# Query projections in two alternating banks, and five loads behind the last output turn of a seam, in a fused transformer block

## The chip, the cores and the metric

The kernel runs on one core of a Trainium2 chip. The metric is device time in microseconds for one execution; the median over several runs is compared. Beside the runs there is one profiled execution, from which all views of the trace come.

## The reference

One transformer block on 2048 tokens of width 1024, in bf16, conditioned by a vector `c` (adaptive layer norm):

```python
mod = (silu(c) @ w_mod).reshape(1, 6, 1, -1)
sa, ca, ga, sb, cb, gb = (mod[:, i] for i in range(6))
h = layernorm(x) * (1 + ca) + sa
x = x + ga * attention(h)        # q = h @ wq, 32 heads of 128; 4 K/V heads, last 512 cached positions; then @ wo
h = layernorm(x) * (1 + cb) + sb
return x + gb * ((silu(h @ w_gate) * (h @ w_up)) @ w_down)     # width 3584 inside
```

## The kernel before

**Stages.** Tokens are cut into four chunks of 512. A start part computes the first two modulation vectors, the first chunk's layer norm and its first queries. Then comes the attention loop over `i`, the running number of chunk and head (128 in all, 32 to a chunk), and at the end of each chunk its output projection. The feed-forward part follows, chunk by chunk. Every instruction is issued from one Python program in the order in which its calls stand; each engine, and SyncE as issuer of nearly all DMAs, works through its own instructions in that order. A small tracker adds the semaphore waits: an instruction waits for the last writer of what it reads, and for the last writer and the readers of what it overwrites. So a DMA written earlier in the program is issued earlier by SyncE, and one that waits holds up all behind it.

**One step of the attention loop.** In step `i` the queries of head `i + 3` are projected (`qproj`, eight matmuls of 512 columns, L672), the scores of head `i - 1` are computed (four matmuls), and the value product of head `i - 2` (`pv`). `qproj` writes PSUM bank `QB` (4); VectorE then copies the bank to SBUF (the CAST, L679). Scores use banks 0 to 3, value products 5 and 6, and bank 7 is `XB`. After `pv` VectorE scales the output (L870, L873) and SyncE transposes it by DMA into `oT_all` (L876); this is called the output's turn. From head 34 on every second head, the even ones, takes another way: scores with queries on the partitions (`nat_scores`, L913 on ScalarE), a normalisation on VectorE (`nat_norm`, L919, L923), a transposing DMA of the probabilities (`nat_turn`, L929) and a value product two steps later (`nat_pv`, copied out by ScalarE, L940).

**The seam.** In the step in which the last head of a chunk is turned (`i` = 33, 65, 97), `oproj` runs the chunk's output projection: eight pieces `k` of 32 matmuls, one for each head, each piece in one of two banks and followed by a residual on VectorE (`resid`, L954 and L956). Piece 0 first takes heads 0 to 23, then the waiting value products, then heads 24 to 31 of the chunk; so head 31's turn has to have landed for the last matmul of piece 0. Into the pieces the first scores of the next chunk are slipped (`between`).

**Late modulation.** The modulation vectors of the feed-forward part are computed one column group at a time: `load_mt(m)` (L597) brings a transposed slice of `w_mod` into one of four slots, `mod_col(m)` (L604, VectorE) multiplies it with the condition and sums. There are 24 such slices. `late_col(m)` is `mod_col(m)` followed by `load_mt(m + 4)`, which has to wait for the slot. The first four loads stand in the table `LOADT` (step: slice), two columns are taken in steps 32 and 33, and `late_cols(k)` takes the rest between the output pieces of chunk 0.

**Other loads on SyncE.** `load_wq` (L363) brings 1 MB of query weights for four heads, `load_x` (L308) 1 MB of tokens for a chunk, by the table `LOADX`.

Of the kernel before, what the change touches and what calls it, by code (L numbers as in the profile page):

```python
# [130 lines left out]
def bass_adaLN_cond__sliding_block_cached__swiglu_ffn__prompt_kernel(  # L131
# [17 lines left out]
    Hq = HD // Dh  # L149
# [112 lines left out]
    QB = 4  # L262
    SCB = 0
    PVB = 5
    XB = 7

    with nc.Block() as block:

        @block.gpsimd
        def _(g):  # L270
# [36 lines left out]
            def load_x(ch):  # L307
                T.op(Q_x[TPC + ch], lambda: SP.dma_start(  # L308
                    x_res[:, ch * TPC:(ch + 1) * TPC, :],
                    xf[ch * CH:(ch + 1) * CH, :].rearrange("(t p) d -> p t d", p=P)),  # L310
                     writes=B_x[ch * TPC:(ch + 1) * TPC])
# [273 lines left out]
            NMT = 4  # L585
# [6 lines left out]
            def load_mt(m):  # L592
                sl = m % NMT
                n = L_ORDER[m]
                if mt[sl] is None:
                    mt[sl] = arena.at(OFF_HT + 2 * sl * KB, [D], BF16, [B_mt[sl]])
                T.op(Q_mt[sl], lambda: SP.dma_start_transpose(  # L597
                    mt[sl].rearrange("p (a b) -> p a b", a=1), w_mod[:, (NF + n) * P:(NF + n + 1) * P]),
                     writes=[B_mt[sl]])
# [8 lines left out]
            def late_col(m):  # L608
                mod_col(m)
                if m + NMT < NL:  # L610
                    load_mt(m + NMT)

            def late_cols(k):
                if k < 7:
                    for m in range(3 * k + (3 if k else 2), 3 * k + 6):
                        late_col(m)
                if k == 3:
                    T.op(DVE, lambda: V.tensor_copy(mstg[:, 0:DT], mcol[:, 2 * DT:3 * DT]), reads=[B_mcol], writes=[B_mstg])
                    row_turn()
                if k == 4:  # L620
                    row_put(2, mrow[0:DT, :], B_mrow)
                if k == 5:
                    row_get(2, rowb[1][:, :], B_row[1])
                if k == 6:
                    for g0 in range(2):
                        mod_take(g0, B_late[g0 + 1])
                    mod_gain(1, B_late[2], B_g[1])
                    for b_ in B_hT[0]:
                        for m_ in B_mt:
                            b_.absorb(m_)  # L630
# [23 lines left out]
            LEAD = 3  # L654
# [8 lines left out]
            def q_slot(i):  # L663
                return NQT + i % 2 if i < NQ0 else i % NQT
# [11 lines left out]
            def qproj(i, b=QB, k0=0):  # L676
                qproj_mm(i, b, k0, DT)
                qs = q_slot(i)
                T.op(DVE, lambda: V.tensor_copy(qT_s[qs], bank(b)), writes=[PB[b], B_qT[qs]])  # L679
# [279 lines left out]
            def oproj_mm(ch, k, b, h0, h1):  # L959
                j, hf = divmod(k, 2)  # L960
                for h in range(h0, h1):
                    mm(bank(b), oT_all[:, h, j * P:(j + 1) * P], wo_s[h // 4][:, h % 4, hf * 512:(hf + 1) * 512],
                       h == 0, h == Hq - 1, [B_wo[h // 4], B_oT[h]], PB[b])
# [6 lines left out]

            def oproj(ch, between, last):
                for k in range(2 * TPC):
                    b = [QB, XB][k % 2]
                    if k == 0:
                        oproj_mm(ch, k, b, 0, Hq - 8)
                        for n in last:
                            nat_pv(n)
                    oproj_mm(ch, k, b, 0 if k else Hq - 8, Hq)
                    oproj_end(ch, k, b)
                    if k < len(between):  # L980
                        between[k]()
                    if ch == 0:
                        late_cols(k)

            ln1 = {}
            ln2 = {}
# [10 lines left out]
                ln2[ch] = ln_task(ch, h2s[s], B_h2[s], 1, 3 * DT, B_late[1])  # L997
                bg.append(ln2[ch])

            LOADX = {19: 2, 2 * Hq + 1: 3}  # L1000
            GATEP = {4: (0, 1), 5: (2,), 6: (3,), 7: (4,), 9: (5,), 10: (6,), 12: (7,), 13: (8,), 15: (9,)}
            GATER = {19 + n: NGP + n for n in range(DT - NGP)}
            GATET = {23: 0, 24: 1}
            GATES = {26: 0, 27: 1}
            PUTT = {22: (0, c_sil, B_csil), 30: (1, mrow[0:DT, :], B_mrow)}
            GETT = {25: (0, sc_row, B_scr), 31: (1, rowb[0][:, :], B_row[0])}
            LOADT = {29: 0, 30: 1, 31: 2, 32: 3}
            LOADO = {5 + (21 * p) // 8: p for p in range(8)}
            LOADK = {1: 1, 5: 2, 6: 3}
            PTAT = {NAT0: OFF_H20, 3 * Hq: OFF_HT}  # L1010
            for i in range(1, NA + 2):
                ch, h = divmod(i, Hq)
                if i in LOADK:
                    load_k(LOADK[i])
                if i == 4:
                    load_wq((i + 4) // 4 + 1)
                if 2 <= i < NQ0:
                    q_shifted(i)
                if i in (2, 3):
                    load_wga(i - 2)  # L1020
                if i in LOADX:
                    load_x(LOADX[i])
                if i in LOADO:
                    load_wo(LOADO[i])
                if i in GATET:
                    gate_turn(GATET[i])
                if i == 28:
                    row_turn()
                if i in PUTT:
                    row_put(*PUTT[i])  # L1030
                if i in GETT:
                    row_get(*GETT[i])
                if i == 7:
                    add_ln1(1)
                if h == 2 and 1 <= ch < NCH - 1:
                    add_ln1(ch + 1)
                if h == 2 and ch == NCH - 1:
                    add_ln2(0)
                if i + LEAD < NA:
                    if (i + LEAD) % Hq == 0:  # L1040
                        finish(ln1[(i + LEAD) // Hq])
                    if i == 1:
                        scores(0)
                    if i in (1, 3, 5):
                        q_bias_mm(i + 1, i + 3, XB)
                    if i > NQ0:
                        qproj(i + LEAD)
                    elif i % 2 == 1:
                        qproj_mm(NQ0 + i // 2, QB, 0, HK)
                    else:  # L1050
                        qproj(NQ0 - 1 + i // 2, QB, HK)
                if i % 4 == 0 and i > NAT0:
                    load_wq(i // 4 + 2)
                if i in (Hq, Hq + 1):
                    late_col(i - Hq)
                n = i - (NA - LEAD)
                if 0 <= n <= 2:
                    oproj_mm(NCH - 1, 0, QB, 8 * n, 8 * n + 8)
                elif n >= 3:
                    oproj_mm(NCH - 1, 1, XB, 8 * (n - 3), 8 * (n - 3) + 8)  # L1060
                seam = (i - 1) % Hq == 0 and i + 1 in NAT
                if i + 1 in PTAT and not seam:
                    pt_region(PTAT[i + 1])
                if i in NAT and (i - 2) % Hq:
                    nat_norm(i, 1)
                nat = i % 2 == 1 and i + 1 in NAT
                if nat and not seam:
                    run_bg(1)
                    nat_scores(i + 1)
                if 1 <= i - 1 < NA and i - 1 not in NAT:  # L1070
                    scores(i - 1)
                if 0 <= i - 2 < NA:
                    if i - 4 in pt_of:
                        nat_pv(i - 4)
                    if i in NAT and (i - 2) % Hq:
                        nat_turn(i)
                    if i - 2 not in NAT:
                        pv(i - 2)
                    if nat and not seam:
                        nat_norm(i + 1, 0)  # L1080
                    ch2, h2 = divmod(i - 2, Hq)
                    if i % 4 == 1 and 5 < i < NAT0:
                        load_wq((i + 4) // 4 + 1)
                    if i in LOADT:
                        load_mt(LOADT[i])
                    if h2 == Hq - 1 and ch2 < NCH - 1:
                        oproj(ch2, [lambda: nat_scores(i + 1), lambda: (nat_norm(i + 1, 0), nat_norm(i + 1, 1))],
                              [n for n in sorted(pt_of) if n // Hq == ch2])
                        if seam:
                            if i + 1 in PTAT:  # L1090
                                pt_region(PTAT[i + 1])
                            nat_turn(i + 1)
                if not nat or seam:
                    run_bg(1)
                for n in GATEP.get(i, ()):
                    gate_part(n)
                if i in GATER:
                    gate_row(GATER[i])
                if i in GATES:
                    gate_sum(GATES[i])  # L1100
                if i == max(GATER):
                    gate_split()
# [107 lines left out]
            for jf in range(NCH * FT):  # L1210
                ch, ft = divmod(jf, FT)
# [45 lines left out]
```

## Time and profile before

| what | us |
|---|---|
| median of three runs | 1270.74 |
| lowest, highest | 1270.41, 1272.22 |
| profiled execution | 1270.27 |
| its span, first to last instruction | 1268.4 |
| outside the span | 1.9 |
| TensorE busy | 1261.8 |
| VectorE, ScalarE, GpSimd busy | 519.9, 392.9, 56.3 |

Busy times are sums over the span and say nothing of where an engine stands still. A row of the timeline gives start, length, engine, line, operation and count of instructions merged into one stretch, and in brackets the idle time before it with what ended it. SPq is the issuing of DMAs by SyncE: its length is the issue, not the transfer. A window's row gives, after its length, each engine's busy time with the count of instructions, then the granted clock of TensorE (1.00 is full speed), the DMA share and GB/s.

### The profile page before, as it was taken

How to read it: one execution, taken by the hardware profiler on the slowest of the kernel's cores; microseconds unless marked ns; L12 is line 12 of the kernel's file. 1: busy time of each engine (PE TensorE's matmuls, PEld its weight loads, DVE VectorE, ACT ScalarE, POOL GpSimd, SP SyncE). 2: the span in 40 equal slices, each digit the busy share in tenths (PEclk: the TensorE clock that was granted, in tenths of full speed). 3: DMA queues.
4: the chain of work that ended last, by engine and by line, in shares of the span. 5: the costliest groups of instructions: out<-in, count | busy, mean ns of one | idle time of the engine just before them, and what ended most of it. 6: DMA issues, size and time to landing. Idle time of an engine off the chain costs nothing.

```text
span 1268.4 us, 17308 instructions
## 1 busy us (share of the span) xinstructions
PE 1261.8 (99%) x7019; PEld 616.7 (49%) x7019; DVE 519.9 (41%) x1081; ACT 392.9 (31%) x718; POOL 56.3 (4%) x95
## 2 busy tenths in 40 slices
PE   9999999999999999999999999999999999999999
PEld 5655445554445554455544444444444444444444
DVE  4676577654246652366422321233212331222222
ACT  4655305775037761177610111011100111011100
POOL 1530000000000000000000000000000000000000
PEclk9999999999999999999999999999999999999999
DMA  9999865987039781098542973055512644035200
GB/s 313 266 265 227 177 129 130 203 167 166 18 57 201 165 185 25 5 208 179 101 141 100 290 240 100 25 158 149 162 46 68 181 142 133 17 123 159 67 9 26
DMA packets 312191, 175.14 MB, mean 138 GB/s; under 512 B 205488, under 2 KB 298032, under 8 KB 312112
## 3 DMA queue, kind: packets, MB, share of 16 engines
q1 hardware_dynamic: 253856, 115.31, 39.6%
q10 hardware_dynamic: 58256, 58.73, 14.5%
q8 instruction: 55, 0.90, 0.3%
q14 instruction: 24, 0.20, 0.1%
HBM read 119.93 MB, written 4.20 MB: 98 GB/s over the span
## 4 chain that ended last, share of the span: by engine, by line
PE 98%; DMA 1%; SPq 1%; DVE 0%; issue 0%
PE ps L277 97%; DMA arena<-arena 1%; DMA arena<-in_w_mod_dram 0%; SPq L597 0%; SPq L315 0%; DVE arena L873 0%; SPq L340 0%; PE ps L281 0%; DVE arena L604 0%; SPq L929 0%; DVE arena L679 0%; SPq L308 0%; DVE arena L502 0%; DVE rl L870 0%; DVE tmp L954 0%
## 5 line engine op out<-in xcount | busy, mean ns | idle before, releaser
L277 PE MATMUL ps<-arena 128*128 128x512 bf16 (+1 forms) x6774 | 1255.6, 348 | 3.8 <-POOL arena L304 2.0
L277 PEld LDWEIGHTS ps<-arena 128*128 128x128 bf16 x6774 | 608.0, 98 | 645.3 <-issue 2.4
L852 ACT ACTIVATE arena<-ps 128x1024 bf16<-128x1024 f32 x160 | 163.7, 1023 | 231.6 <-PE ps L277 224.3
L1185 ACT ACTIVATE arena<-ps 128x512 bf16<-128x512 f32 x112 | 66.9, 597 | 501.0 <-PE ps L277 501.0
L1186 DVE TENSOR_TENSOR arena<-ps,arena 128x512 bf16<-128x512 f32 x112 | 77.5, 692 | 276.2 <-PE ps L277 276.2
L954 DVE TENSOR_TENSOR tmp<-ps,rowb 128x512 f32<-128x512 f32 (+1 forms) x65 | 44.4, 683 | 291.9 <-PE ps L277 291.9
L679 DVE CAST arena<-ps 128x512 bf16<-128x512 f32 x120 | 82.9, 691 | 75.9 <-PE ps L277 75.9
L913 ACT ACTIVATE arena<-ps 128x512 bf16<-128x512 f32 x96 | 56.8, 595 | 27.6 <-PE ps L277 23.2
L913 ACT ACTIVATE tmp<-ps 128x512 bf16<-128x512 f32 x92 | 54.5, 595 | 18.8 <-PE ps L277 13.4
L873 DVE TENSOR_TENSOR arena<-ps,rl 128x512 bf16<-128x512 f32 x81 | 56.0, 691 | 3.0 <-DVE rl L870 0.2
L435 POOL TENSOR_SCALAR rstd<-mv 128x1 f32<-128x1 f32 x28 | 6.1, 216 | 910.0 <-DVE mv L434 910.0
L870 DVE RECIPROCAL rl<-ps 128x4 f32<-128x4 f32 x81 | 14.8, 183 | 71.8 <-PE ps L277 71.6
L430 DVE BATCH_NORM_STATS2 st<-x_res 128x6 f32<-128x512 bf16 x62 | 42.4, 684 | 3.5 <-DMA x_res<-in_A_x_dram 3.4
L923 DVE TENSOR_SCALAR arena<-arena,pinv 128x512 bf16<-128x512 bf16 x96 | 33.9, 353 | 3.4
L940 ACT ACTIVATE arena<-ps 128x512 bf16<-128x512 f32 x47 | 27.8, 592 | 19.6 <-PE ps L277 19.6
L923 DVE TENSOR_SCALAR tmp<-tmp,pinv 128x512 bf16<-128x512 bf16 x92 | 32.5, 353 | 3.3
L604 DVE SCALAR_TENSOR_TENSOR arena<-arena 128x1024 bf16<-128x1024 bf16 x24 | 29.3, 1222 | 1.6
L956 DVE TENSOR_TENSOR arena<-tmp,x_res 128x512 bf16<-128x512 f32 (+2 forms) x33 | 22.3, 676 | 1.1
L956 DVE TENSOR_TENSOR x_res<-tmp,x_res 128x512 bf16<-128x512 f32 x32 | 22.2, 692 | 1.1
L446 DVE TENSOR_SCALAR arena<-arena,gain,mod_bf 128x512 bf16<-128x512 bf16 x56 | 21.2, 421 | 0.0
L441 DVE TENSOR_SCALAR nsc<-x_res,mv,rstd 128x1024 bf16<-128x1024 bf16 x30 | 19.2, 641 | 0.0
L913 ACT ACTIVATION_READ_ACCUMULATOR arena<-ps 128x1 f32 x96 | 18.8, 196 | 0.0
(67 smaller groups left out, 150.9 us busy)
## 6 DMA issues: line engine op xcount, KB each, us to landing
arena<-in_A_wq_dram SPq DMA_DIRECT2D x30, 1024.0 KB, 6.0
arena<-in_B_w_gate_dram ACTq DMA_DIRECT2D x28, 1024.0 KB, 5.3
arena<-in_B_w_up_dram ACTq DMA_DIRECT2D x28, 1024.0 KB, 7.9
arena<-in_A_wo_dram SPq DMA_DIRECT2D x8, 1024.0 KB, 7.5
arena<-in_B_w_down_dram SPq DMA_DIRECT2D x7, 1024.0 KB, 8.7
out_dram<-arena SPq DMA_DIRECT2D x15, 256.0 KB, 2.0
x_res<-in_A_x_dram SPq DMA_DIRECT2D x3, 1024.0 KB, 6.8
arena<-in_w_mod_dram SPq DMA_DIRECT2D x8, 256.0 KB, 6.5
```

Of the source, the lines that this page charges most:

```text
L277: T.op(PE, lambda: TE.matmul(out_ap, lhsT, rhs, start=start, stop=stop, skip_group_check=skip), reads=reads, writes=[bank_buf])
L430: T.op(DVE, lambda: V.bn_stats(st_[sl][:, hf * 6:hf * 6 + 6], x_res[:, t, hf * 512:hf * 512 + 512]), reads=[B_x[t]], writes=[B_st[sl]])
L604: T.op(DVE, lambda: V.scalar_tensor_tensor(mt[sl], mt[sl], 1.0, sc_row, op0=ALU.mult, op1=ALU.mult, accum_out=mcol[:, n:n + 1]), reads=[B_ ...
L679: T.op(DVE, lambda: V.tensor_copy(qT_s[qs], bank(b)), writes=[PB[b], B_qT[qs]])
L852: T.op(ACT, lambda: A.activation(ex_s[es][:, 2 * kp:2 * kp + 2, :], banks2(SCB + 2 * kp), AF.Exp, scale=att_scale), writes=[PB[SCB + 2 * k ...
L873: T.op(DVE, lambda: V.tensor_tensor(o_s[os_].rearrange("p (a b) d -> p a b d", a=2), psap(PVB * 512, [[512, 2], [130, 2], [1, P]]), rlb, A ...
L913: T.op(ACT, lambda: A.activation(pn[s][:, j * 512:(j + 1) * 512], bank(SCB + j), AF.Exp, scale=att_scale, accum_out=psum[s][:, j:j + 1]), ...
L923: T.op(DVE, lambda: V.tensor_scalar(pj, pj, pinv[s][:, j:j + 1], None, op0=ALU.mult), reads=[B_pinv[s][hf]], writes=[B_pn[s][hf]])
L954: T.op(DVE, lambda: V.tensor_tensor(tmp[s][:, 0:n], bank(b, n), rowb[ri][:, c0:c0 + n], ALU.mult), reads=[B_row[ri]], writes=[PB[b], B_tmp ...
L956: T.op(DVE, lambda: V.tensor_tensor(dst[:, c0:c0 + n], tmp[s][:, 0:n], x_res[:, t, c0:c0 + n], ALU.add), reads=[B_tmp[s], B_x[t]], writes= ...
L1185: T.op(ACT, lambda: A.activation(sg_s[ss], bank(gb), AF.Silu), writes=[PB[gb], B_sg[ss]])
L1186: T.op(DVE, lambda: V.tensor_tensor(guT[:, ft, :], bank(ub), sg_s[ss], ALU.mult), reads=[B_sg[ss]], writes=[PB[ub], B_gu[ft]])
```

## The change

Three things are moved; no instruction is added or removed.

1. `qproj` takes banks in turn: `XB` in even steps, `QB` in odd ones. `oproj` begins with `XB` in place of `QB`, so that its piece 0 does not use the bank of the queries just projected.
2. The first four late loads come one step earlier (steps 28 to 31). The columns in steps 32 and 33 are taken without a load behind them; loads 4 and 5 are issued at the beginning of chunk 0's output projection, behind the last output turn and the query weights' load of that step.
3. The last tokens (`load_x(3)`) are loaded in the output projection of chunk 1, behind its piece 1, in place of the beginning of step 65.

```diff
             def oproj(ch, between, last):
                 for k in range(2 * TPC):
-                    b = [QB, XB][k % 2]
+                    b = [XB, QB][k % 2]
                     if k == 0:
+                        if ch == 0:
+                            load_mt(NMT)
+                            load_mt(NMT + 1)
                         oproj_mm(ch, k, b, 0, Hq - 8)
...
                     if ch == 0:
                         late_cols(k)
+                    if ch == 1 and k == 1:
+                        load_x(3)
...
-            LOADX = {19: 2, 2 * Hq + 1: 3}
+            LOADX = {19: 2}
...
-            LOADT = {29: 0, 30: 1, 31: 2, 32: 3}
+            LOADT = {28: 0, 29: 1, 30: 2, 31: 3}
...
                     if i > NQ0:
-                        qproj(i + LEAD)
+                        qproj(i + LEAD, [XB, QB][i % 2])
...
                 if i in (Hq, Hq + 1):
-                    late_col(i - Hq)
+                    mod_col(i - Hq)
```

## The prediction

> **What bounds the kernel now.** I read the page's busy times and chain first, then the waits of the TensorE, then the timeline at the places that the chain names.
>
> ```profile
> PE 1261.8 (99%) x7019; PEld 616.7 (49%) x7019; DVE 519.9 (41%) x1081; ACT 392.9 (31%) x718; POOL 56.3 (4%) x95
> PE 98%; DMA 1%; SPq 1%; DVE 0%; issue 0%
> PE ps L277 <- POOL arena L304: 2.0, 1, 2.0
> PE ps L277 <- DMA arena<-arena: 1.2, 2, 0.7
> ...
> ```
>
> The first two rows are the page's engines and the chain by engine: the TensorE is the bound for 98% of the span, and nothing the diff does takes a matmul away. The next two are from the list of the TensorE's waits: total, times, longest. The first is the start of the kernel, and so are the two rows left out. Only the second, two waits for a transposing DMA with 1.2 us in sum, lies at places that the change touches. So the question is how much of this goes, whether there is idle time that the waits don't count, and whether something new is late.
>
> The page says that ends of matmuls are modelled, so I measure idle time from starts. The pace comes from a stretch of the feed-forward part where only matmuls of 512 columns run, the row being a window with its busy times and counts:
>
> ```profile
> 800.00:1000.00 200.00, 200.00 (x928) 90.73 (x927) 56.65 (x94) 20.89 (x35) 4.63 (x12) 1.00 0.37 112
> ```
>
> 200 us by 928 is 0.216 us a matmul. Now the timeline of the TensorE around five spots (start, length of the merged stretch, count, idle time before it):
>
> ```profile
> 144.80 0.38 PE L277 MATMUL ps<-arena 128*128 128x512 bf16 x1
> 145.83 0.60 PE L277 MATMUL ps<-arena 128*128 128x512 bf16 x2 [0.66 <-DMA arena<-arena]
> 204.42 1.42 PE L277 MATMUL ps<-arena 128*128 128x512 bf16 x5
> 311.99 0.81 PE L277 MATMUL ps<-arena 128*128 128x512 bf16 x3
> 313.38 0.82 PE L277 MATMUL ps<-arena 128*128 128x512 bf16 x3 [0.57 <-DMA arena<-arena]
> 364.76 1.55 PE L277 MATMUL ps<-arena 128*128 128x512 bf16 x6
> 531.14 1.77 PE L277 MATMUL ps<-arena 128*128 128x512 bf16 x7
> ```
>
> A matmul alone is shown as 0.38 us long, so n of them at full pace take (n-1) x 0.216 + 0.38.
>
> - Seam after the first chunk: 145.83 - 144.80 = 1.03, less one pace: 0.81 us lost.
> - Seam after the second: the third matmul behind 311.99 starts at 312.42, the next at 313.38: 0.96 less 0.216 is 0.74 lost.
> - 204.42: five should take 1.24 and take 1.42: 0.18 lost.
> - 364.76: six should take 1.46, take 1.55: 0.09. 531.14: seven should take 1.68, take 1.77: 0.09.
>
> Together 1.91 us. The last three are invisible to the list of waits, since the modelled ends cover them.
>
> **The change, part 1: the last output turn first.** The chain shows what the first two losses hang on (start, length, what):
>
> ```profile
> 138.74 0.70 DVE arena L873
> 139.74 1.30 SPq L597
> 141.08 1.30 SPq L597
> 142.42 3.36 DMA arena<-arena
> 306.08 0.77 SPq L929
> 306.90 0.57 SPq L308
> 307.56 5.77 DMA arena<-arena
> ```
>
> At seam 0, head 31's output is ready at 138.74 + 0.70 = 139.44, but SyncE first issues the rest of head 30's turn and two late weight loads (L597), 1.30 each. The turn goes out at 142.42 and lands 3.36 later, at 145.78; the output projection's matmul of head 31 would have started at 145.83 - 0.81 = 145.02. In the changed kernel the first four late loads come one head earlier, and loads 4 and 5 behind the last turn and the query weights' load. Head 30's turn then follows the load that now starts at about 135.74:
>
> ```profile
> 135.74 1.31 SPq L597 DMA_TRANSPOSE arena<-in_w_mod_dram  x1
> 144.62 0.53 SPq L363 DMA_DIRECT2D arena<-in_A_wq_dram  x1
> ```
>
> so it goes at 137.1 and takes 1.3, and SyncE is free at 138.4, before 139.44. Head 31's turn is issued at 139.5 and by the old 3.36 lands at 142.9, 2.1 us in time; it may take 5.5 before anything is lost. So 0.81 is gained; what covers the turn is the 31 matmuls ahead of head 31's, from about 138.3.
>
> At seam 1 the 1 MB token load (L308) leaves its place ahead of head 63's turn. The turn of probabilities (L929) stays ahead, so the issue moves from 307.56 to 306.90 only. The nearest row is the same seam a chunk later, where no token load stands: there, of the DMA issues in 474.45 to 476, the answer is
>
> ```profile
> arena<-arena SPq DMA_TRANSPOSE x1, 3.8
> 474.50 1.92 SPq L876 DMA_TRANSPOSE arena<-arena  x1
> ```
>
> and by 3.8 the turn lands at 310.7. Needed is 313.38 - 0.74 = 312.64, that is at most 5.7 us. Even with the old 5.77 it would be 0.03 to 0.07 late. Bounds of the gain 0.67 and 0.74; I take 0.74. What is next late here is head 62, whose copy on ScalarE
>
> ```profile
> 311.33 0.60 ACT L940 ACTIVATE arena<-ps 128x512 bf16<-128x512 f32 x1 [7.47 <-PE ps L277]
> ```
>
> ends at 311.93; its matmul starts at 312.42, so there is 0.5 us to spare and nothing moves it.
>
> **Part 2: what the moved loads may cost.** The first load goes to SyncE one head earlier, behind head 26's turn:
>
> ```profile
> 121.98 4.69 SPq L876 DMA_TRANSPOSE arena<-arena  x2
> 126.76 0.97 SPq L363 DMA_DIRECT2D arena<-in_A_wq_dram  x1
> 127.77 2.27 SPq L597 DMA_TRANSPOSE arena<-in_w_mod_dram  x1
> ```
>
> The two turns in the first row are 1.2 long each and the rest is free, so the load fits and delays nobody; its buffer, the first chunk's normalised tokens, was last read by the query projection just before. Loads 4 and 5 go out later: after the turn (139.5 + 1.2) and the query weights' load (0.53), so at about 141.3 and 142.6, against 137.09 and 141.08 now. Who waits for them is VectorE's modulation columns, in order, the first two of these rows:
>
> ```profile
> 150.33 1.23 DVE L604 SCALAR_TENSOR_TENSOR arena<-arena 128x1024 bf16<-128x1024 bf16 x1
> 151.67 1.23 DVE L604 SCALAR_TENSOR_TENSOR arena<-arena 128x1024 bf16<-128x1024 bf16 x1
> 154.03 0.69 DVE L954 TENSOR_TENSOR tmp<-ps,rowb 128x512 f32<-128x512 f32 x1 [1.12 <-PE ps L277]
> 160.93 0.69 DVE L954 TENSOR_TENSOR tmp<-ps,rowb 128x512 f32<-128x512 f32 x1
> DMA to landing us min/median/max: 3.1/3.7/5.9
> ```
>
> The last row is that of all 24 late loads (the group of L597). By its worst, 5.9, loads 4 and 5 land at 147.2 and 148.5; they are wanted at 149.5 and 150.9, the old times less 0.81. Should they be late, VectorE stops, and behind it stands the residual of output piece 1 (154.03). Its bank is written again by piece 3, at about 160.9 (piece 2's residual starts at 160.93), so up to 6 us of delay is still covered by piece 2's 32 matmuls. I cost this at nothing; bounds 0 and 0.
>
> The token load, now issued directly behind head 63's turn because SyncE waits for nothing there, is first read by the layer norm of chunk 3, a chunk later: nothing. A turn with a 1 MB load right behind it is in the trace; it is alone in the DMA issues of 299.9 to 301.25:
>
> ```profile
> arena<-arena SPq DMA_TRANSPOSE x1, 2.4
> 301.29 0.53 SPq L363 DMA_DIRECT2D arena<-in_A_wq_dram  x1
> ```
>
> **Part 3: two banks for queries.** No instruction is added; the query projection alternates between bank 7 and bank 4, so its first matmul no longer waits for the CAST of the head before. Where a value product stands between, that wait is never late. It is late only in the second head behind a seam, which has just the four score matmuls in between. The weight-load rows name it:
>
> ```profile
> 365.49 3.55 PEld L277 LDWEIGHTS ps<-arena 128*128 128x128 bf16 x29 [0.41 <-DVE arena L679]
> 532.09 1.84 PEld L277 LDWEIGHTS ps<-arena 128*128 128x128 bf16 x10 [0.41 <-DVE arena L679]
> 204.19 0.69 DVE L679 CAST arena<-ps 128x512 bf16<-128x512 f32 x1
> ```
>
> The third row's cast ends at 204.88, the late matmul starts at about 205.03. It also waits for the next query weights, landed long ago, so I take the whole 0.18 and keep 0.09 as its low end. Gain 0.18 + 0.09 + 0.09 = 0.36, lower bound 0.27. The output pieces swap banks as well, so at a seam piece 0 meets a bank that was emptied a head ago, and piece 7's bank is next wanted two heads on.
>
> **The sum.** 0.81 + 0.74 + 0.36 = 1.91, bounds 1.75 and 1.91. The profiled execution took 1270.27 with a span of 1268.4; its changed counterpart would take 1268.36 with a span of 1266.5. The median of the runs is 0.47 higher, 1270.74, so the forecast is 1268.83, or 1268.8: 0.15% faster. About 0.2%, 2.5 us, is what a measurement of this kernel can tell from no change, so this is a gain inside that bound.
>
> **The rivals.**
>
> A, more than the profile shows. The three runs lie between 1270.41 and 1272.22, and the seam waits depend on when a DMA lands; if the median's 0.47 is more of that wait, it goes too: 1268.36, and a third of a microsecond of scatter below it is past the bound of 1268.2. For it: the turns' landings vary a lot. Against: nothing shows where the 0.47 lies. 0.34 for a time below 1268.2.
>
> B, the turn at seam 0 stays late because SyncE is not free at 138.4; only seam 1 and the banks pay: 1270.74 - 1.10 = 1269.6. Against: every issue there is a row above. 0.04.
>
> C, slower: at seam 1 the token load, now behind the turn, takes DMA engines from it. The extremes of the turns (the group of L876) are
>
> ```profile
> DMA to landing us min/median/max: 2.4/2.7/8.9
> ```
>
> With 8.9 it lands at 315.8, the wait becomes 3.2 instead of 0.74, and 1.17 gained elsewhere leaves +1.3: 1272.0. The stall begins at 5.7 and eats the whole gain from 7.6. Against: the 2.4 above with such a load behind. "DMA: Bandwidth & Descriptors" of the Trainium skill, section "Two DMAs through the same engine are not ordered", says nothing orders transfers across engines, which speaks for it; the 2.4 speaks against. 0.06, of which 0.04 past +0.2%.
>
> D, slower: the granted clock falls as the query projection changes banks each head. A hundredth less over 200 to 566 us, where the change acts, would cost 3.7 us, 1272.5 with the gain taken off.
>
> ```profile
> 200.00:566.00 366.00, 365.41 (x2129) 183.33 (x2127) 187.54 (x461) 188.94 (x404) 8.52 (x22) 1.00 0.61 128
> ```
>
> The clock there is 1.00, though scores go through four banks and value products through two already. "TensorE: Matmul & The Clock Gate" of the Trainium skill, section "A second HAM failure mode: psum-queue depth-cycling", reports a kernel whose cycling through banks left TensorE idle so often that its clock swung; by that rule this change is harmful. The 1.00 disagrees with it. 0.04.
>
> **How the numbers follow.** Forecast 0.52, A 0.34, B 0.04, C 0.06, D 0.04. Faster by over 0.2% is A: 0.34. Slower is D and most of C: 0.08. The rest, 0.58, is within. The range goes from 1267.8 (A's 1268.36 less twice the 0.3 by which the fastest run lies below the median) to 1270.4, B's time with 0.8 of scatter such as the highest run suggests; outside lie C, D and the far end of A.
>
> **What would show it right or wrong.** Right: the waits hold no arena<-arena DMA for the TensorE; at the first seam L876 comes directly before L363 and the two L597; the span is near 1266.5; no stretch behind 204, 364 and 531 is longer than its count allows. Wrong: a wait for L604 or a residual in the TensorE's list near 150 to 165, a clock below 1.00, or the wait at 313 still there.

## The result, and the profile after

The changed kernel takes 1268.03 us in the median of 14 runs (1267.64 to 1269.98), against 1271.24 for 14 runs of the kernel before beside it (1269.83 to 1272.22). The ratio is 0.9978, 95% interval 0.9970 to 0.9987: faster by 0.13 to 0.30%. A ratio of 1 lies outside that interval, and its middle, 0.22%, is just past the 0.2% that the prediction set as a bound. The forecast was 1268.8 within 1267.8 to 1270.4; it was counted from 1270.74, the median of three runs, 0.5 below that of the 14 here. Below, the median and the ratio of e5 leave out one execution, the profiled one, which took 7677 us.

The page of the changed kernel, its busy times and its chain, and then the list of TensorE's waits (total, times, longest):

```profile
span 1266.6 us, 17280 instructions
PE 1261.1 (100%) x7019; PEld 617.1 (49%) x7019; DVE 519.3 (41%) x1081; ACT 393.1 (31%) x718; POOL 56.1 (4%) x95
PE 99%; DVE 0%; POOL 0%; issue 0%; POOLq 0%
```

```profile
PE ps L277 <- POOL arena L304: 2.0, 1, 2.0
PE ps L277 <- DVE arena L502: 0.6, 1, 0.6
PE ps L277 <- DVE arena L679: 0.3, 1, 0.3
```

The span is 1.8 us shorter with 0.7 us less TensorE busy time and the same number of matmuls; DMA has left both the chain and the list of waits. The timeline of TensorE at the five spots of the prediction:

```profile
143.75 2.97 PE L277 MATMUL ps<-arena 128*128 128x512 bf16 x13
202.76 3.40 PE L277 MATMUL ps<-arena 128*128 128x512 bf16 x15
309.82 4.48 PE L277 MATMUL ps<-arena 128*128 128x512 bf16 x20
362.70 3.62 PE L277 MATMUL ps<-arena 128*128 128x512 bf16 x16
529.15 3.19 PE L277 MATMUL ps<-arena 128*128 128x512 bf16 x14
```

By the rule of the prediction, (n-1) x 0.216 + 0.38, these should take 2.97, 3.40, 4.48, 3.62 and 3.19: nothing is lost at any of them. What SyncE issues around the two seams (start, length of the issue), and the DMA issues of 139.5 to 140.5 and of 306.2 to 306.4 with their time to landing:

```profile
136.43 1.31 SPq L597 DMA_TRANSPOSE arena<-in_w_mod_dram  x1
137.78 3.12 SPq L876 DMA_TRANSPOSE arena<-arena  x2
141.00 0.53 SPq L363 DMA_DIRECT2D arena<-in_A_wq_dram  x1
141.57 5.09 SPq L597 DMA_TRANSPOSE arena<-in_w_mod_dram  x2
306.29 1.22 SPq L876 DMA_TRANSPOSE arena<-arena  x1
307.56 0.57 SPq L308 DMA_DIRECT2D x_res<-in_A_x_dram  x1
```

```profile
arena<-arena SPq DMA_TRANSPOSE x1, 2.4
arena<-arena SPq DMA_TRANSPOSE x1, 2.5
```

The order is the predicted one: turn, query weights, two late loads; and turn, tokens. Both turns land 2.4 to 2.5 us after their issue, where before they took 3.4 and 5.8.

One loss is larger than before. It is in the start part, which the change does not touch; the timeline of TensorE there:

```profile
44.80 0.79 PE L277 MATMUL ps<-arena 128*128 128x129 bf16 x11
45.88 1.47 PE L277 MATMUL ps<-arena 128*128 128x512 bf16 x6 [0.30 <-DVE arena L679]
```

From the starts of the matmuls 0.46 us are lost at this spot, against 0.13 in the profile before. That is why the span is 1.8 shorter and not 2.1. In the three profiles of the changed order (this one, e7 and e8) the loss here is 0.19 to 0.46 us, in the eight of the others that have the same start part 0 to 0.30; the last section shows what it goes with.

### The profile page after: what moved, and what is told of

It reads as the page before. It is cut to its first block, busy times and chain, and to the rows that moved or that the text cites. A ratio compares the mean times of both kernels' runs of the same rounds, so it can differ in the third digit from the quotient of the medians.

```text
span 1266.6 us, 17280 instructions
## 1 busy us (share of the span) xinstructions
PE 1261.1 (100%) x7019; PEld 617.1 (49%) x7019; DVE 519.3 (41%) x1081; ACT 393.1 (31%) x718; POOL 56.1 (4%) x95
## 4 chain that ended last, share of the span: by engine, by line
PE 99%; DVE 0%; POOL 0%; issue 0%; POOLq 0%
PE ps L277 99%; PE ps L281 0%; DVE arena L705 0%; DVE arena L873 0%; DVE arena L679 0%; POOL arena L304 0%; DVE arena L502 0%; DVE tmp L954 0%; POOL arena L300 0%; DVE arena L956 0%; POOL arena L299 0%; DVE rl L870 0%; DVE gain_f L492 0%; PE ps L516 0%; POOLq L300 0%
```

## The experiments

Losses below are taken from starts of neighbouring matmuls less the pace, as in the prediction, after the first 30 us.

**The kernel before, a second profile (e1).** No edit.

> The kernel before, unchanged, profiled a second time. Theory (the seam waits are fixed by the order of SyncE's issues): the profile shows the same losses of TensorE as the first one, 0.8 us at 145, 0.7 us at 313, and 0.1 to 0.2 at 205, 305, 365 and 532, each within 0.15; span 1268 to 1269. Rival (the waits depend on when a DMA lands and are longer in most runs than in the first profile): one of the two DMA waits differs by over 0.3 us. Time ratio 1.000 within its interval.

Measured: 1271.24 us, ratio 1.0002 (0.9993 to 1.0011), span 1268.7. TensorE's timeline at the first seam:

```profile
143.76 0.81 PE L277 MATMUL ps<-arena 128*128 128x512 bf16 x3
146.05 1.25 PE L277 MATMUL ps<-arena 128*128 128x512 bf16 x5 [1.47 <-DMA arena<-arena]
```

The last of the three starts at 144.19; 146.05 less that, less a pace, is 1.64 us lost, twice as much as the 0.82 in the first profile. At 313 it is 0.74 again, and at 205, 305, 365 and 532 it is 0.18, 0.13, 0.09 and 0.09. So the rival holds for the first seam: its wait depends on the run. The turn itself landed only 0.2 us later than in the first profile (146.0 against 145.8); TensorE was at head 31's matmul 0.6 us earlier (144.4 against 145.0, the starts less the losses), so time saved ahead of the seam came back as waiting. Over all the profiles here with the old order, it was 0.82, 1.64, 0.95, 0.99 and 1.10 (mean 1.1) at the first seam and 0.61 to 1.11 (seven profiles, mean 0.8) at the second.

**The banks alone (e2).**

```diff
-                    b = [QB, XB][k % 2]
+                    b = [XB, QB][k % 2]
...
-                        qproj(i + LEAD)
+                        qproj(i + LEAD, [XB, QB][i % 2])
```

> Only the banks of the query projection and of the output pieces are changed. Theory: the losses at 205, 365 and 532 (0.18, 0.09, 0.09) go, and so does the short wait ahead of the output projection at 305 and 472 (0.13, 0.04), which hung on the CAST of the query bank too; 0.53 us in all, span near 1267.9; the two DMA waits at 145 and 313 stay at 0.8 and 0.7. Rival (the waits for the CAST were covered): the span does not move beyond 0.1 us apart from the start part.

Measured: 1270.72 us, ratio 0.9996 (0.9987 to 1.0004), span 1267.8. The time alone can't tell this from nothing, but the profile can: the losses at 205, 305, 365, 472 and 532, 0.53 us together, are all gone, and only the two DMA waits are left after 30 us:

```profile
PE ps L277 <- POOL arena L304: 2.0, 1, 2.0
PE ps L277 <- DMA arena<-arena: 1.5, 2, 0.8
PE ps L277 <- DVE arena L502: 0.6, 1, 0.6
```

**The late loads alone (e3)**

```diff
+                        if ch == 0:
+                            load_mt(NMT)
+                            load_mt(NMT + 1)
...
-            LOADT = {29: 0, 30: 1, 31: 2, 32: 3}
+            LOADT = {28: 0, 29: 1, 30: 2, 31: 3}
...
-                    late_col(i - Hq)
+                    mod_col(i - Hq)
```

> Only the late weight loads are moved. Theory: the wait at 145 (0.82 us) goes and nothing else; span near 1267.6. Rival (DMA engines are saturated around this seam, so that the order of issues does not matter): a wait of over 0.4 us for an arena<-arena DMA stays at 145.

**and the last tokens alone (e4).**

```diff
-            LOADX = {19: 2, 2 * Hq + 1: 3}
+            LOADX = {19: 2}
...
+                    if ch == 1 and k == 1:
+                        load_x(3)
```

> Only the last token load is moved. Theory: the wait at 313 (0.74 us) goes and nothing else; the turn of head 63 lands 2.4 to 3.8 us after its issue; span near 1267.7. Rival (the load takes DMA engines from the turn although it is issued behind it): the turn takes over 5.7 us to land and a wait stays.

Measured: e3 1269.82 us, 0.9991 (0.9982 to 1.0000); e4 1270.09 us, 0.9993 (0.9984 to 1.0002). In e3 the loss at 145 is gone, in e4 that at 313, where the turn lands 2.5 us after its issue with the 1 MB behind it; the others stay. The spans, 1268.4 and 1268.2, missed the expectation by 0.8 and 0.5, since in both TensorE waited for something that no edit touches. Its waits in e4:

```profile
PE ps L277 <- POOL arena L304: 2.0, 1, 2.0
PE ps L277 <- DMA arena<-arena: 0.8, 1, 0.8
PE ps L277 <- DMA arena<-in_A_wq_dram: 0.6, 1, 0.6
...
```

That is the query weights of head 32, at 121: 0.81 us lost in e4, 0.59 in e3, 0.01 or nothing in the two profiles before and the one after. The three parts together come to 0.04 + 0.09 + 0.07 = 0.20%, as much as the whole change within its interval. By time alone none of the three can be told from nothing, since each interval reaches 1.0000 or beyond; it is the profiles that show what each does.

**Only the queries alternate (e5, and e10 for its profile).**

```diff
-                        qproj(i + LEAD)
+                        qproj(i + LEAD, [XB, QB][i % 2])
```

> Only the queries alternate between two banks; the output pieces keep their old order, so that their last piece leaves from bank 7 and the next query projection goes straight to bank 7. Theory (the two halves of the bank edit need each other): that projection now waits for the residual's read of the bank, about 0.2 + 0.7 us behind the last matmul, at three seams: a new loss of 0.8 to 1.1 us each, near 196 (or 203), 363 and 530, 2.4 to 3.3 in all; the losses at 205, 365, 532 (0.35 together) go, those at 145, 305 and 313 stay; 2 to 3 us slower than before. Rival (the residual is covered by what stands between): no new loss, 0.35 us faster.

> Only the queries alternate, once more, for its profile. Theory: three new losses of 0.8 to 1.1 us, at the first query projection behind each of three seams, named as a wait for VectorE's line 954; together with the 0.35 that goes away this is the 2 to 3 us by which the timed runs were slower. Rival (the time was lost elsewhere): no wait for line 954 in TensorE's list.

Measured: 1273.6 us in ten runs of e5, ratio 1.0019 (1.0010 to 1.0028), slower; the single run of e10 took 1273.1. The list of TensorE's waits in e10, and its timeline at the first of the new places:

```profile
PE ps L277 <- DVE tmp L954: 2.4, 3, 0.8
...
PE ps L277 <- DMA arena<-arena: 1.9, 2, 1.0
...
```

```profile
194.77 0.59 PE L277 MATMUL ps<-arena 128*128 128x512 bf16 x2
196.15 1.04 PE L277 MATMUL ps<-arena 128*128 128x512 bf16 x4 [0.79 <-DVE tmp L954]
```

0.95 us are lost at 196, 365 and 532 each, 2.85 in all, while the 0.35 of the CAST goes: 2.5 net, and 0.19% of 1271 is 2.4. The swap of the output pieces is therefore no detail. Without it the last piece leaves from the bank that the next query projection wants.

**Only load 5 behind the turn (e6).**

```diff
+                        if ch == 0:
+                            load_mt(NMT + 1)
...
-                    late_col(i - Hq)
+                    (late_col if i == Hq else mod_col)(i - Hq)
```

> Only load 5, the one that stands directly ahead of the last output turn of the first chunk, is moved behind it; the others keep their places. Theory (there is a deadline, and the turn has only to be issued by about 141.5): the turn goes out near 141.1, lands near 144, and the wait at 145 is gone entirely, with half of the edit. Rival (each load ahead of the turn costs its 1.3 us): a wait of 0.2 to 0.9 us remains at 145.

Measured: 1270.14 us, 0.9992 (0.9983 to 1.0001); in the profile 0.82 us are still lost at 145, so my theory fell. The wait lies in the rival's range, but not for its reason, since 1.3 us less in front of the turn gained next to nothing. SyncE's issues, TensorE, and the landings of the load at 140.05 and of the turn at 141.39:

```profile
140.05 1.30 SPq L597 DMA_TRANSPOSE arena<-in_w_mod_dram  x1
141.39 1.27 SPq L876 DMA_TRANSPOSE arena<-arena  x1
```

```profile
145.62 0.60 PE L277 MATMUL ps<-arena 128*128 128x512 bf16 x2 [0.65 <-DMA arena<-arena]
```

```profile
arena<-in_w_mod_dram SPq DMA_TRANSPOSE x1, 5.1
```

```profile
arena<-arena SPq DMA_TRANSPOSE x1, 4.2
```

The turn was issued 1.0 us earlier than before and landed at 145.6, 0.2 earlier than before (145.8). It came 0.4 behind the load ahead of it, which landed at 145.2. Before it was the same: that load was issued at 141.08, took 4.2 and landed at 145.3, the turn 0.5 later. So the turn lands behind the transfer ahead of it in the queue, whenever it is issued itself. Why that transfer took 5.1 us here is taken up in the last section.

**Loads 3 and 5 behind the turn (e11)**, load 4 still ahead of the turn before.

```diff
+                        if ch == 0:
+                            load_mt(NMT - 1)
+                            load_mt(NMT + 1)
...
-            LOADT = {29: 0, 30: 1, 31: 2, 32: 3}
+            LOADT = {29: 0, 30: 1, 31: 2}
...
-                    late_col(i - Hq)
+                    (late_col if i == Hq else mod_col)(i - Hq)
```

> The kernel before, with loads 3 and 5 behind the first chunk's last output turn; load 4 stays where it is, ahead of the turn before it, and the first loads keep their steps. New theory (the turn lands about 0.4 us behind the late load just ahead of it in the queue, whenever it is issued itself): with no load between the last two turns it lands 2.4 to 3.3 us after its issue near 139.6 and the wait at 145 is gone; moving the first loads a step earlier is not needed for it. Rival (the queue is still too full with load 4 in front): a wait of over 0.3 us at 145.

Measured: 1269.46 us, 0.9988 (0.9979 to 0.9997). The loss at 145 is gone. The two turns' landings, of the issues at 138.58 and at 139.9:

```profile
138.58 2.57 SPq L876 DMA_TRANSPOSE arena<-arena  x2
```

```profile
arena<-arena SPq DMA_TRANSPOSE x1, 4.7
```

```profile
arena<-arena SPq DMA_TRANSPOSE x1, 3.8
```

Head 30's turn, right behind load 4, lands at 143.2, head 31's at 143.7. The 3.8 is more than the 2.4 to 3.3 expected. For head 31's turn the theory gives the reason, as it lands 0.5 behind the transfer ahead; for head 30's it does not, as load 4 had landed at 141.3, 1.9 before it (see the last section). Taking the load between the two turns away is enough; the early start of the first loads, which the change also has, is not needed for this wait.

**Late loads still later (e7).** The changed kernel, with loads 4 and 5 behind load 7.

```diff
-                        if ch == 0:
-                            load_mt(NMT)
-                            load_mt(NMT + 1)
...
                         late_col(m)
+                        if m == 3:
+                            load_mt(NMT)
+                            load_mt(NMT + 1)
```

> The changed kernel with loads 4 and 5 put behind load 7, which waits for a modulation column, so that both land some 6 to 7 us later (near 155 and 156 instead of 148 and 149) and VectorE stands still for their columns about 4 to 5 us. Theory (VectorE has 6 us before an output piece waits for its bank): VectorE's idle time near 152 grows by 4 us or more, the residual of piece 1 moves from 153.5 to near 157.5, and TensorE has no wait there; same time as the changed kernel. Rival (the chain of late columns is close to critical): a new wait of TensorE for a residual between 153 and 195.

Measured: 1268.4 us, 0.9977 (0.9968 to 0.9986), like the changed kernel. VectorE and TensorE in its timeline (line 957 is here the residual's first half):

```profile
154.36 1.23 DVE L604 SCALAR_TENSOR_TENSOR arena<-arena 128x1024 bf16<-128x1024 bf16 x1 [5.39 <-DMA arena<-in_w_mod_dram]
156.85 0.69 DVE L957 TENSOR_TENSOR tmp<-ps,rowb 128x512 f32<-128x512 f32 x1
```

VectorE stands still for 5.4 us, the residual of piece 1 starts at 156.85 instead of 153.45, and no matmul is late: the only loss in this profile is 0.19 us at 45. So a residual that is 3.4 us late costs nothing; the rest of the 6 us was not tried.

**The changed kernel, a second profile (e8).** No edit.

> The changed kernel, profiled a second time. Theory (after 30 us only two places still depend on the luck of a run: the query CAST at 46, and the query weights of head 32 that land close to 121): no loss anywhere else over 0.05 us; at 46 between 0.1 and 0.5, at 121 between 0 and 0.8; ratio to before 0.9978. Rival (the gain hung on one lucky profile): a wait at 145 or 313 is back.

Measured: 1268.11 us, 0.9975 (0.9964 to 0.9985). Losses after 30 us: 0.31 at 46, 0.16 at 121, nothing else. So in both profiles of the changed kernel 0.46 to 0.47 us are left, against 2.2 and 2.9 in those of the kernel before.

**Two more places (e9)**

```diff
-                if 2 <= i < NQ0:
+                if 2 <= i < NQ0 and i % 2 == 1:
                     q_shifted(i)
...
+                if i == 25:
+                    load_wq(8)
                 if i in GETT:
...
+                if 2 <= i < NQ0 and i % 2 == 0:
+                    q_shifted(i)
...
-                    if i % 4 == 1 and 5 < i < NAT0:
+                    if i % 4 == 1 and 5 < i < NAT0 and i != 25:
```

> The changed kernel with two more moves: in even steps 2 to 6 the shifted query is written behind the CAST and not ahead of it on VectorE, and the query weights of heads 32 to 35 are issued at the beginning of step 25, ahead of a row read and an output turn. Theory: the loss at 46 (0.1 to 0.5) and the one at 121 (0 to 0.8) are gone, the weights land 2 to 3 us earlier; 0.3 to 1 us faster than the changed kernel in the median, ratio to before 0.997 to 0.9975. Rival (the moved writes come late elsewhere): a new wait of TensorE for VectorE's line 705 or for a DMA between 40 and 125, no gain.

**and the tokens of chunk 2 as well (e12).**

```diff
-            LOADX = {19: 2}
+            LOADX = {}
...
+                    if ch == 0 and k == 6:
+                        load_x(2)
```

> The kernel of both mended places, with the 1 MB of tokens of chunk 2 also moved, from step 19 into the output projection of chunk 0 behind its piece 6. Theory (the waits for query weights at 107 and 121 come from too many bytes asked for between 90 and 120): the weights for head 28 land 2 us or more earlier, no wait of TensorE after 32 us is over 0.1 us; ratio to before 0.996 to 0.9975. Rival (their landing is set by latency, not by bytes): the weights land as before and a wait at 107 or 121 can appear.

Measured: e9 1267.90 us, 0.9970 (0.9958 to 0.9981); e12 1267.88 us, 0.9971 (0.9960 to 0.9981). In e9 the losses at 46 and 121 are gone, but, as its rival has it, a new one of 0.72 us stands at 107, in front of head 28's query weights, which were issued at 98.3 and took 8.5 us:

```profile
106.88 1.47 PE L277 MATMUL ps<-arena 128*128 128x512 bf16 x6 [0.55 <-DMA arena<-in_A_wq_dram]
```

```profile
arena<-in_A_wq_dram SPq DMA_DIRECT2D x1, 1024.0 KB, 8.5
```

In e12 the same load, issued at 98.26, takes 5.7 and lands 2.9 us earlier, as the theory of too many bytes has it; the tokens had also stood ahead of it in SyncE's queue, and the run does not tell the two apart. After 32 us its profile has no loss at all; all of TensorE's waits are now in the start:

```profile
PE ps L277 <- POOL arena L304: 2.0, 1, 2.0
PE ps L277 <- DVE arena L502: 0.5, 1, 0.5
PE ps L281 <- DVE nsc L441: 0.5, 2, 0.3
```

Against the changed kernel the medians gain 0.1 to 0.2 us, less than the 0.3 to 1 expected of e9, and these runs don't separate it from nothing. What is visible is the spread: eight runs of e12 lie between 1267.67 and 1268.03, those of the changed kernel between 1267.64 and 1269.98.

## Why the prediction was right, and where its steps were off

**The sum.** Each of the five terms went as worked out: nothing is left at any of the five spots. The sum was too small in two places. The first seam's 0.81 came from one profile, which showed the shortest wait of five; their mean is 1.1. And a sixth spot was overlooked: at the second and third seam piece 0's first matmul waited for the CAST in the query bank too, 0.13 and 0.04 us at 305 and 472, which the edit of part 3 takes away (e2). The text says of the swapped pieces only that they meet an emptied bank. With these, 1.1 + 0.8 + 0.35 + 0.17 is 2.4 us from the profiles. The interval of the ratio gives 1.7 to 3.8 us; its middle, 2.8, is 0.4 above what the profiles account for, and whether that is anything stays open. The 0.2% that the prediction took for the smallest change that can be told from none was too coarse: the interval here reaches 0.09% to either side.

**Part 1, the step that failed.** "By the old 3.36 lands at 142.9; it may take 5.5" treats the landing as a delay of the turn's own from its issue. e6 shows that this is wrong: issued 1.0 earlier but still behind a load, the turn lands only 0.2 earlier. The result came out right because no load is left between the last two turns and head 30's has landed by 140.9; head 31's then takes 2.4 and lands at 142.1. In e11, where head 30's lands only at 143.2, it takes 3.8. The same holds at the second seam, where the prediction kept "the old 5.77" as a bad end: before, the turn landed at 313.3, 0.5 behind the tokens; with the tokens gone from in front it took 2.5, 0.5 behind the turn of probabilities that landed at 308.3. The gain there was therefore the whole 0.74.

**Part 2.** Loads 4 and 5 landed 6.2 and 4.7 us after their issues at 141.57 and 143.93, at 147.8 and 148.7, against 147.2 and 148.5 estimated, and VectorE wanted the first at 149.76. Of the 6 us of cover behind that, e7 used 3.4 without a loss; where the cover ends was not tried.

**Part 3.** The losses at 205, 365 and 532 were the CAST's, with 0.18 whole at 205. The half-sentence about the output pieces' swap is worth more than the gain: e10.

**The rivals.** A was at work: all four other profiles with the old order at the first seam lose more there than the first one, and the median ratio 0.9978 lies on A's side of the bound, its interval on both. So the forecast's 0.15%, held to be the likelier, was too small, though within the range. B did not happen. C is ruled out for this kernel: with 1 MB right behind it the turn took 2.5 us in the changed kernel and in e4. "DMA: Bandwidth & Descriptors" of the Trainium skill, section "Queues, rings and completion order", says that each engine takes its descriptors in ring order; e6's 0.4 us between load and turn agrees with that, and the warning of the section cited for C had no effect here. D is ruled out as well: the granted clock is 1.00 in every profile with alternating banks.

## What to carry to other kernels

When an engine is busy for 99% of the span, measure its lost time from start to start of neighbouring instructions: 0.53 us of the gain here, five waits for a CAST, never appeared in the list of waits. A small transfer on which the bounding engine waits has to be issued with nothing large or late right ahead of it in its queue; giving it an earlier place in time helps little while something stands in front, and what followed it cost it nothing here (2.5 us with 1 MB right behind). And banks that are used in turn have to be in step across the border of two stages, or the gain comes back with the other sign (2.5 us slower in e5).

## What was not expected of the hardware

The turn's landing. With the way free it comes 2.4 us after the issue; otherwise 0.4 to 0.6 us behind the transfer issued just ahead of it, even where its own issue was over a microsecond earlier than in another run. Of the 1053 output turns in the thirteen profiles other than e5's, 923 land within 0.3 us of the later of these two times, and the other 130 land later still. What goes with that are the packets of the queues that the profile calls "instruction" (program code, by that name). Of 223 turns with such a packet in flight in the 1.5 us before that time, 117 land later; of the 830 others only 13, each of them right behind a row read (L652). At the first seam of e6 the packet is one of 16 KB from 142.7 to 143.6. Beside it 28 packets of 256 B, started at 142.7 to 142.9, end only at 144.4 to 144.5, where such packets mostly take 0.02 us. The activity of the DMA engines from 142 to 145 us, in 40 slices, and that packet:

```profile
DMA  9999999999999000000000000010000069999959
q8 instruction: 1, 0.02, 1.9%
```

The load and the turn of e6 were both under way then. By the 4.2 and 3.9 us of the two late loads before it, the load would have landed by 144.2 and the turn 0.4 behind it, ahead of TensorE at 144.8. This is an estimate, and by it e6's expectation fell because of the code as much as of the queue. The late landing of head 30's turn in e11 goes with such a packet too (141.2 to 142.3). In the changed kernel the packet comes at 142.0, just as the turn lands at 142.1. No run moved the code, so how much of the wait at 145 it makes is not shown.

The jitter of the start part. The shifted query on VectorE (L705) takes 0.48 us in some places and up to 1.57 (e7) in others of the same size; in the changed kernel's timeline the long one lies under a GpSimd instruction:

```profile
38.15 0.48 DVE L705 TENSOR_SCALAR arena<-arena,bq 128x512 bf16<-128x512 f32 x1
43.67 1.27 POOL L811 TENSOR_TENSOR arena<-arena 128x512 f32<-128x512 f32 x1
43.81 1.41 DVE L705 TENSOR_SCALAR arena<-arena,bq 128x512 bf16<-128x512 f32 x1
```

GpSimd's ends at 44.94, VectorE's at 45.22, and the CAST behind it makes TensorE late by 0.46. It is not this case alone. Of the 104 such instructions in the same thirteen profiles, the 57 that no GpSimd instruction overlaps took 0.48 to 0.49 us; 21 under one took no more than 0.52; the 26 that took longer all lie under one; and all 15 that started while the GpSimd addition of the second row (L811, L814 in e7) ran, or 0.02 us ahead of it, ended 0.28 us behind its end. "SBUF — State Buffer" of the Trainium skill, section "SBUF: two separate sides", describes a port pair that GpSimd and, for some of its instructions, VectorE hold in turns for a whole instruction. The 0.28 fits that, but whether the shifted query is one of these instructions no view here tells, and no run took the GpSimd instruction away.
